# Loads around the attentions' ends moved from SyncE's to ScalarE's DMA queue, output weights in one transfer, all engines in a new order

## The chip, the cores and the metric

The kernel runs on one core of a Trainium2 chip. The metric is the device time of one execution in microseconds. The time before is 1257.52 us, the median of 3 runs (1256.28 to 1263.55). The chip's engines have their own instruction queues and run side by side: PE (TensorE, matmuls), DVE (VectorE), ACT (ScalarE), POOL (GpSimd) and SP (SyncE, which here only issues DMAs). Each engine takes its instructions in the order in which they stand.

## The reference

The reference is one block of a speech encoder with two branches, and the gradients of all its inputs. B = 2 batches, T = 4000 tokens, D = 144 channels, bfloat16.

```python
xa = layernorm(x)
q, k, v = split(xa @ w_qkv)
glob = softmax(q @ k.T * D**-0.5) @ v @ w_att_out
u, g = split(gelu(xa @ w_mlp_in))
loc = (u * depthwise5(layernorm(g), dw_csgu)) @ w_mlp_out
m = concat(glob, loc)
out = x + (m + depthwise5(m, dw_merge)) @ w_merge
# and the gradients of x and of the seven weights for a given grad_out
```

The attention is full: 4000 x 4000 scores in each batch, of which the kernel needs the softmax P and, for the gradients, dP and dS.

## The kernel before

**Tiles.** The tokens of a batch are cut into 32 tiles of 125 queries. `phase_att` runs once for each batch. For tile t it makes the scores in four chunks of 1000 keys (PE, L1046 and L1052), their minimum on the way out of PSUM (DVE, L1070), the exponential (ACT, L1078), the same for dP, which leaves PSUM with a cast on ACT (L1091) and a multiplication on DVE (L1093), or by DVE alone (L1088). P and dS are transposed by DMAs that SP issues: one of P for a whole tile (L1082, called P_tr below) and two halves of dS (L1265). Products with them follow on PE: Y (L1102, from the transposed P), Z (L1140, from the transposed dS) and X (L1185, from both untransposed; DVE adds its results up at L1191). Behind each tile ACT stores a row block of Y and of Z in DRAM (L1117 to `Yn_d`, L1145 to `Zn_d`). The local branch's forward and backward work goes in pieces between the tiles and stores `ug_d` (L633).

**The ends of the attentions.** After the last tile of a batch, class `Merge` does what needs all tokens. `open_early` loads the incoming gradient with its neighbours (`go_h2`) and the stored rows `Yg0` (attention branch) and `Yg1` (local branch); `late_y` loads the last 8 rows of `Yg0` and, in batch 0, starts batch 1's input x; `rem_rows` fills two small stacks `Yr0` and `Yr1`; `open_late` loads `Zn`; `late_w` loads the fused output weights `VU` (two tiles) and `VUs` (two tiles stored once, loaded four times each at shifted positions, over memsets). Matmuls follow:

- `Hps0`, `Hps1` (L1467): the gradient of the merge taps, 384 matmuls; they use the PSUM of the score chunks, and so wait for the last chunks to be read.
- `pz` (L1567): 64 matmuls on `Zn`.
- `po` (L1589, L1591): the output, from `VU`, `VUs` and transposes of Y (SP: L1527, L1535, L1544).
- `dx_a`, `dx_b` (L1604 on ACT, L1618 to L1622): the gradient of x.

In batch 0 the next batch's layernorm, projections and first tiles run into this. I call it the **middle end** (about 535 to 670 us). In batch 1 class `Final` makes the weight gradients at the same time: the **final end** (1125 us to the end).

**Order.** Tables of numbers, one for each engine (`ORDER`, L744 on), set the order of instruction groups; `plan` chains the groups of an engine in that order. SP and ACT each have a DMA queue. All their DMAs share eight semaphores in turn, by the place in the program (named DMAHW0 to DMAHW7 in the rows below): a DMA is issued only when the one eight places earlier that has its semaphore has landed, whichever queue issued that. An engine that waits so holds all that stands behind it.

Of the kernel before, what the change touches and what calls it, by code (L numbers as in the profile page):

```python
# [15 lines left out]
D = 144  # L16
DR = 16
# [94 lines left out]
def end_weights(k, W, pool):  # L112
    eng = k.nc.sync
    W.Wqkv = load_k_(k, pool, k.w_qkv, 0, 3 * D, "Wqkv_e", eng)
    W.Wo = load_k_(k, pool, k.w_att_out, 0, D, "Wo_e", eng)
    W.Wm = [load_k_(k, pool, k.w_merge, h * D, D, "Wm_e%d" % h, eng) for h in range(2)]
    W.Wl = load_k_(k, pool, k.w_mlp_out, 0, D, "Wl_e", eng)
    W.Wvo = unspill(k, pool, W.Wvo_d, "Wvo_e", eng)


def end_taps(k, W, pool):
    eng = k.nc.sync
# [4 lines left out]
class Head:  # L127
# [12 lines left out]
    def wt(self, q, shape):  # L140
        return self.areas[q].tile(shape, BF)
# [153 lines left out]
    def vu(self, h):  # L295
# [4 lines left out]
        if h == 0:  # L300
            W.VU, W.VUs = [], []
# [3 lines left out]
        v = wt(3, [128, 5, D])  # L305
# [6 lines left out]
        W.VU.append(spill(k, v, "VU_d%d" % h))  # L312
        sr = wt(3, [128, 2, 80])
        for ch in range(2):
            for kk in range(5):
                nc.gpsimd.tensor_scalar(sr[:, ch, kk * DR:(kk + 1) * DR], WT[h][:, ch, 128:D], W.cols[:, 2 * h + ch, kk:kk + 1], 1.0, op0=ALU.mult, op1=ALU.mult)
        vs = wt(1, [80, D])
        pt = self.ps([128, D], F32)
        for ch in range(2):
            nc.tensor.matmul(pt[0:80, :], sr[:, ch, :], self.Wm[h][:, ch, :], start=(ch == 0), stop=(ch == 1))  # L320
        nc.scalar.copy(vs, pt[0:80, :])
        W.VUs.append(spill(k, vs, "VUs_d%d" % h))
# [421 lines left out]
for _s in """  # L744
PE 10 1 1 1 1 1 1 1 1 1 1 1 1 1 1 1 1 1 1 1 1 1 1 1 1 1 1 1 1 1 1 1 1 1 1 1 1 1 1 1 1 1 1 1 1 1 1 1 1 1 1 1 1 1 1 1 1 1 1 1 1 1 1 1 1 1 1 1 1 1 1 1 1
# [1337 lines left out]
```

## Time and profile before

| what | before |
|---|---|
| median of 3 runs | 1257.52 us |
| profiled execution | 1252.05 us |
| its span | 1250.3 us |
| PE busy | 1175.9 us (94%) |
| DVE busy | 1042.8 us (83%) |
| ACT busy | 719.9 us (58%) |
| POOL busy | 439.4 us (35%) |
| granted TensorE clock, mean | 0.981 |
| SP's queue, share of 16 DMA engines | 90.9% |
| ACT's queue, share of 16 DMA engines | 2.9% |

The profiled execution's own time is 1.75 us more than its span, and 5.47 us less than the median of the runs. Busy time says little of a single stage: the views used below cut the span into stretches, and name for each wait who waited, for whom and how long. DMA issues have a duration of their own on the queue that issues them (SPq, ACTq), which is not the duration of the transfer.

### The profile page before, as it was taken

How to read it: one execution, taken by the hardware profiler on the slowest of the kernel's cores; microseconds unless marked ns; L12 is line 12 of the kernel's file. 1: busy time of each engine (PE TensorE's matmuls, PEld its weight loads, DVE VectorE, ACT ScalarE, POOL GpSimd, SP SyncE). 2: the span in 40 equal slices, each digit the busy share in tenths (PEclk: the TensorE clock that was granted, in tenths of full speed). 3: DMA queues.
4: the chain of work that ended last, by engine and by line, in shares of the span. 5: the costliest groups of instructions: out<-in, count | busy, mean ns of one | idle time of the engine just before them, and what ended most of it. 6: DMA issues, size and time to landing. Idle time of an engine off the chain costs nothing. (4 is left out here: it accounts for less than half of the span.)

```text
span 1250.3 us, 37996 instructions
## 1 busy us (share of the span) xinstructions
PE 1175.9 (94%) x15384; PEld 923.3 (74%) x15384; DVE 1042.8 (83%) x2846; ACT 719.9 (58%) x1281; POOL 439.4 (35%) x913
## 2 busy tenths in 40 slices
PE   9899999999999999978598999999999999998988
PEld 7566777777777777778576777777777777776877
DVE  7688989898989898856567999989998989896565
ACT  4765666656666665525546666665656556564451
POOL 7543434333443343304124344343433333342100
PEclk9899999999999999989799999999999999999989
DMA  6888899999999999998879999999899999999892
GB/s 133 160 150 148 155 166 162 164 160 164 162 162 162 160 164 164 180 203 161 165 122 164 159 173 156 179 161 164 151 170 156 162 153 162 166 160 182 182 174 75
DMA packets 720027, 200.64 MB, mean 160 GB/s; under 512 B 708365, under 2 KB 716042, under 8 KB 719845
## 3 DMA queue, kind: packets, MB, share of 16 engines
q1 hardware_dynamic: 694326, 190.84, 90.9%
q10 hardware_dynamic: 25348, 7.13, 2.9%
q8 instruction: 120, 1.97, 0.7%
q14 instruction: 57, 0.46, 0.1%
q0 software_dynamic: 176, 0.25, 0.1%
HBM read 22.52 MB, written 16.53 MB: 31 GB/s over the span
## 5 line engine op out<-in xcount | busy, mean ns | idle before, releaser
L1078 ACT ACTIVATE Pb<-Pb,nm 125x1000 bf16<-125x1000 bf16 x256 | 275.2, 1125 | 116.7 <-DVE nm L1072 111.6
L1070 DVE TENSOR_SCALAR_CACHE_REDUCE Pb<-ps 125x1000 bf16<-125x1000 f32 x256 | 306.1, 1196 | 42.5 <-PE ps L1052 40.0
L1185 PE MATMUL X<-SX 125*128 125x144 bf16 x2048 | 292.5, 227 | 0.9 <-ACT l_sq L551 0.7
L1185 PE MATMUL X<-SX,Pb 125*128 125x144 bf16 x2048 | 290.9, 226 | 0.8 <-POOL SX L1131 0.6
L1091 ACT CAST SX<-ps 125x1000 bf16<-125x1000 f32 x189 | 188.1, 995 | 161.7 <-PE ps L1052 158.1
L1046 PE MATMUL ps<-xaT_m,qt 128*128 128x500 bf16 x1024 | 261.1, 375 | 7.7 <-DVE Pb L1070 4.3
L1191 DVE TENSOR_TENSOR acc<-X,acc 125x432 f32<-125x432 f32 x372 | 201.1, 550 | 22.2 <-PE X L1185 21.0
L1185 PEld LDWEIGHTS <-SX 125*128 125x128 bf16 x2048 | 197.6, 98 | 28.2 <-issue 28.2
L1185 PEld LDWEIGHTS <-Pb 125*128 125x128 bf16 x2048 | 200.5, 98 | 2.0 <-issue 1.4
L1140 PE MATMUL yz<-xa_aug,SX 125*128 125x144 bf16 x2048 | 151.0, 228 | 8.2 <-DMA SX<-SX 7.1
L1102 PE MATMUL yz<-xa_aug,SX 125*128 125x145 bf16 x2048 | 144.7, 228 | 10.1 <-DMA SX<-Pb 10.1
L1046 PEld LDWEIGHTS <-qt 128*128 128x128 bf16 x1024 | 91.8, 98 | 71.4 <-issue 8.9
L1102 PEld LDWEIGHTS <-SX 125*128 125x128 bf16 x2048 | 133.4, 98 | 12.7 <-DMA SX<-Pb 11.5
L1140 PEld LDWEIGHTS <-SX 125*128 125x128 bf16 x2048 | 133.2, 98 | 12.7 <-DMA SX<-SX 9.7
L1093 DVE TENSOR_TENSOR SX<-SX,Pb 125x1024 bf16<-125x1024 bf16 x189 | 133.6, 710 | 10.2 <-ACT SX L1091 6.5
L1052 PEld LDWEIGHTS <-qt 16*128 16x128 bf16 x1024 | 26.4, 91 | 110.3 <-issue 110.3
L1052 PE MATMUL ps<-XR,qt 16*128 16x500 bf16 x1024 | 102.9, 380 | 0.0
L1088 DVE TENSOR_TENSOR SX<-ps,Pb 125x1000 bf16<-125x1000 f32 x67 | 79.9, 1193 | 1.2 <-PE ps L1052 1.0
L553 POOL TENSOR_SCALAR l_a<-l_sq 125x576 bf16<-125x576 bf16 x32 | 21.8, 681 | 143.7 <-ACT l_sq L551 143.4
L1129 POOL TENSOR_SCALAR g<-qz,rl 125x144 f32<-125x144 bf16 x62 | 24.9, 401 | 103.2 <-DVE rl L1109 93.7
L1467 PE MATMUL Hps<-Yg,go_h 125*128 125x144 bf16 x640 | 52.7, 232 | 8.6 <-DMA Yg<-Yn_d 8.6
L658 POOL TENSOR_SCALAR l_w<-gdr,nc,c 125x144 f32<-125x144 bf16 x64 | 32.6, 514 | 75.9 <-DVE nc L654 56.5
(593 smaller groups left out, 2041.0 us busy)
## 6 DMA issues: line engine op xcount, KB each, us to landing
go_h<-in_grad_out_dram SPq DMA_DIRECT2D x4, 567.0 KB
go_d<-in_grad_out_dram SPq DMA_DIRECT2D x8, 281.2 KB
Yn_d<-yn ACTq DMA_DIRECT2D x64, 35.2 KB
Zn_d<-qz ACTq DMA_DIRECT2D x64, 35.2 KB
ug_d<-ugr ACTq DMA_DIRECT2D x32, 70.3 KB
out_dram<-Pb SPq DMA_DIRECT2D x16, 140.6 KB
SX<-in_x_dram SPq DMA_DIRECT2D x16, 140.6 KB
out_dram<-SX SPq DMA_DIRECT2D x16, 140.6 KB
```

The lines of the kernel that those rows point to most:

```text
L1046: mm = nc.tensor.matmul(pp[r // 2][:, r % 2, 0:CH], QT[i][:, 3 * h, :], xaTm[:, c * CH:(c + 1) * CH], start=True, stop=False)
L1052: nc.tensor.matmul(pp[r // 2][:, r % 2, 0:CH], QT[i][rs, 1 + h, :], xr, start=False, stop=True)
L1070: nc.vector.tensor_scalar(pv(Pbuf, i % NPB, c2), src, -1.0, 3.0e38, op0=ALU.mult, op1=ALU.min, accum_out=NM[i][:, c2:c2 + 1])
L1078: nc.scalar.activation(v, v, ACT.Exp, bias=NM[i][:, 4:5], scale=-1.0)
L1088: nc.vector.tensor_tensor(pv(Sbuf, i % NDB, c2), src, pv(Pbuf, i % NPB, c2), op=ALU.mult)
L1091: nc.scalar.copy(pv(Sbuf, i % NDB, c2), src)
L1093: nc.vector.tensor_tensor(sc, sc, pchunk(i % NPB, c2), op=ALU.mult)
L1102: nc.tensor.matmul(Y, PT[0:PB, j, :], xaa[:, j, 0:D + 1], start=(j == 0), stop=(j == NB - 1))
L1140: nc.tensor.matmul(Z, ST[0:PB, j, :], xaa[:, j, 0:D], start=(j == 0), stop=(j == NB - 1))
L1185: nc.tensor.matmul(X[:, jj, :], l, r, start=(n_ == 0), stop=(n_ == len(ops) - 1))
L1191: nc.vector.tensor_tensor(av, X[0:PB, 0:nj, :], av, op=ALU.add)
L1467: nc.tensor.matmul(H[a // 6][0:rows, a // 3 % 2, (a % 3) * D:(a % 3 + 1) * D], lhs, self.src[h][:, j, :], start=(j == 0 and a % 3 == 0), s ...
```

## The change

Six places take ScalarE's queue where they took SyncE's: the weights for the final products (`end_weights`, `end_taps`), the loads of `open_early`, `late_y` (with batch 1's x) and `open_late`, and batch 1's gradient. The DMA transposes, the four small copies of `rem_rows`, output stores and copies between DRAM buffers stay on SyncE. The output weights become one tile and one transfer: the kernel's head now computes the shifted copies of `VUs` with four matmul pairs of 128 rows out of a zeroed tile, puts them behind `VU` in one tile for each half and stores that; at each end one load of 128 x 2592 elements (648 KB) takes the place of two loads of 180 KB, eight of 23 KB and two memsets. The order tables of all engines are new.

```diff
 def end_weights(k, W, pool):
-    eng = k.nc.sync
+    eng = k.nc.scalar
 ...
 def end_taps(k, W, pool):
-    eng = k.nc.sync
+    eng = k.nc.scalar
 ...
-        v = wt(3, [128, 5, D])
+            W.VA = k.tc.dram_tile([128, 2, 9, D], BF, name="VA_d")
+            self.va, self.sr = wt(3, [128, 9, D]), wt(3, [128, 2, 232])
+            nc.gpsimd.memset(self.sr, 0.0)
+        v, sr = self.va, self.sr
 ...
-        vs = wt(1, [80, D])
-        pt = self.ps([128, D], F32)
-        for ch in range(2):
-            nc.tensor.matmul(pt[0:80, :], sr[:, ch, :], self.Wm[h][:, ch, :], start=(ch == 0), stop=(ch == 1))
-        nc.scalar.copy(vs, pt[0:80, :])
-        W.VUs.append(spill(k, vs, "VUs_d%d" % h))
+        for q in range(2):
+            pt = self.ps([128, 2 * D], F32)
+            for r in range(2):
+                o = 48 - DR * (2 * q + r)
+                for ch in range(2):
+                    nc.tensor.matmul(pt[:, r * D:(r + 1) * D], sr[:, ch, o:o + 128], self.Wm[h][:, ch, :], start=(ch == 0), stop=(ch == 1))
+            nc.scalar.copy(vf[:, (5 + 2 * q) * D:(7 + 2 * q) * D], pt[:])
+        nc.sync.dma_start(W.VA[:, h], v)
 ...
 # one line of the order tables, before and after (all tables are new)
-Pool 425 -262 23 254 -250 -2 -8 -43 52 -50 298 -297 299 2 -303 40 248 -245 30 -32 68 -4 -56 -44 40 -42 85 -41 9 -2 4 237 -238 -2 245 -151 4 -18 20 1
+Activation 148 1 -4 -1 2 5 -1 -3 81 1 2 1 13 -11 7 -5 14 1 -14 129 -128 1 13 23 10 4 -9 1 80 -78 82 -5 2 -49 46 -36 -5 40 -39 8 37 -7 -36 18 5 19 -15
 ...
     def open_early(self):
 ...
-        eng = nc.sync
+        eng = nc.scalar
 ...
     def late_y(self):
 ...
-        eng = k.nc.sync
+        eng = k.nc.scalar
 ...
     def late_w(self):
-        for h in range(2):
-            self.k.nc.sync.dma_start(self.VU[h], self.W.VU[h][:])
-            self.k.nc.gpsimd.memset(self.VUs[h], 0.0)
-            for r in range(4):
-                self.k.nc.sync.dma_start(self.VUs[h][DR * r:DR * r + 80, r, :], self.W.VUs[h][:])
+        self.k.nc.scalar.dma_start(self.VA, self.W.VA[:])
 ...
-            load_tok(k, self.Zn, 16 * g, S.Zn_d, 16 * g, 16 * g + 16, nc.sync)
+            load_tok(k, self.Zn, 16 * g, S.Zn_d, 16 * g, 16 * g + 16, nc.scalar)
 ...
-    pre_load_go(k, 1, S1, [nc.sync])
+    pre_load_go(k, 1, S1, [nc.scalar])
```

In the rows below, lines of code stand two higher in the changed kernel (L1084 is L1082 before) up to about L1450, and three lower behind it. SP's queue has 605 rows before and 512 after, ACT's 1297 and 1358.

SP around the last transposition of P in the middle end (the row at L1082, or L1084 after), before:

```order
L1265 DMA_TRANSPOSE SX_102<-SX_102 128x16x128 [waits DMAHW5_49,DVE_49,Activation_49]
L51 DMA go_h2_10322<-in_grad_out_dram 112x2592 [waits DMAHW7_49,Pool_49]
L1154 DMA_TRANSPOSE zt_10364<-qz_103 128x2x128 [waits DMAHW0_49]
L42 DMA Yg0_10312<-Yn_d0_79 112x16x144 [waits DMAHW1_49]
L51 DMA go_h2_10322<-in_grad_out_dram 12x2592 [waits DMAHW2_49]
L51 DMA go_h2_10322<-in_grad_out_dram 12x2592 [waits DMAHW4_49]
L1082 DMA_TRANSPOSE SX_102<-Pb_101 128x32x128 [waits DMAHW5_49,PE_49,Activation_49]
L51 DMA go_h2_10322<-in_grad_out_dram 112x2592 [waits DMAHW6_49]
L42 DMA Pb_101<-in_x_dram 112x1152 [waits DMAHW7_49]
```

And after:

```order
L1156 DMA_TRANSPOSE zt_10376<-qz_103 128x2x128 [waits DMAHW7_49,DVE_49]
L1267 DMA_TRANSPOSE SX_102<-SX_102 128x16x128 [waits DMAHW0_49,DVE_49,Activation_49]
L1084 DMA_TRANSPOSE SX_102<-Pb_101 128x32x128 [waits DMAHW1_49,DMAHW6_49,PE_49,Activation_49]
L1578 DMA SX_102<-in_x_dram 125x576 [waits DMAHW5_49,PE_49,Pool_49]
L396 DMA go_d1_85<-in_grad_out_dram 1000x1x144 [waits DMAHW6_49]
L1267 DMA_TRANSPOSE SX_102<-SX_102 128x16x128 [waits DMAHW7_49,DVE_49,PE_49]
L1436 DMA Yr1_10333<-ug_d0_80 124x2x16 [waits DMAHW0_49,Pool_49]
L1436 DMA Yr0_10332<-Yn_d0_79 124x2x16 [waits DMAHW1_49,Pool_49]
```

The four plain loads between a transposition of dS and that of P have left SP.

ACT at the same place. The last cast of a dP chunk (`ps_10381` before, `ps_10393` after) releases `Hps1`'s PSUM and the last half of dS. Before:

```order
L1091 CAST SX_102<-ps_10351 125x8x125 [waits DMAHW3_49,PE_49]
L1078 ACTIVATE Pb_101<-Pb_101,nm_10086 125x8x125
L1117 DMA Yn_d0_79<-yn_10266 125x144 [waits DMAHW4_49,Activation_49]
L1145 DMA Zn_d0_78<-qz_103 125x144 [waits DMAHW6_49]
L1091 CAST SX_102<-ps_10381 125x8x125 [waits PE_49]
L1159 COPY zt_10568<-pt_10569 128x256 [waits PE_49]
```

After, the last 12 of the 24 rows behind the cast of the chunk ahead, up to this cast:

```order
L51 DMA go_h2_10334<-in_grad_out_dram 112x2592 [waits DMAHW0_49]
L42 DMA Pb_101<-in_x_dram 112x1152 [waits DMAHW1_49]
L51 DMA go_h2_10334<-in_grad_out_dram 12x2592 [waits DMAHW2_49]
L1119 DMA Yn_d0_79<-yn_10278 125x144 [waits DMAHW3_49,Activation_49]
L42 DMA Yg0_10324<-Yn_d0_79 112x8x144 [waits DMAHW4_49]
L43 DMA Pb_101<-in_x_dram 13x1152 [waits DMAHW5_49]
L43 DMA Yg1_10325<-ug_d0_80 13x16x144 [waits DMAHW6_49]
L1147 DMA Zn_d0_78<-qz_103 125x144 [waits DMAHW4_49]
L42 DMA Pb_101<-in_grad_out_dram 112x1152 [waits DMAHW5_49,PE_49]
L43 DMA Pb_101<-in_grad_out_dram 13x1152 [waits DMAHW6_49]
L43 DMA Pb_101<-in_grad_out_dram 13x1152 [waits DMAHW7_49]
L1093 CAST SX_102<-ps_10393 125x8x125 [waits PE_49]
```

Two stores stood between the last two casts on ACT before; 23 transfers do after, each with its wait for a landing.

ACT behind the last row block of Z in the middle end, after (these loads stood on SP before, among transposes):

```order
L42 DMA Yg0_10324<-Yn_d0_79 112x8x144 [waits DMAHW5_49,DMAHW1_49]
L43 DMA Yg0_10324<-Yn_d0_79 13x8x144 [waits DMAHW2_49]
L1451 DMA SX_102<-VA_d_986 128x2592 [waits DMAHW3_49,PE_49]
L1147 DMA Zn_d0_78<-qz_103 125x144 [waits DMAHW4_49,DVE_49]
L42 DMA Pb_101<-Zn_d0_78 112x2304 [waits PE_49]
L43 DMA Pb_101<-Zn_d0_78 13x2304 [waits DMAHW6_49]
L1161 COPY zt_10713<-pt_10714 128x256 [waits PE_49]
```

The last rows of `Yg0`, the output weights and the first half of `Zn` now stand around the store of Z's last row block (L1147), in one run of transfers.

More of the change, by code (lines that the diff above doesn't have):

```diff
@@ L300, in vu @@
         if h == 0:
-            W.VU, W.VUs = [], []
             W.sWm_d = [spill(k, sWm[q], "sWm_d%d" % q) for q in range(2)]
@@ L311, in vu @@
             nc.scalar.copy(vf[:, q * 360:(q + 1) * 360], pt[:])
-        W.VU.append(spill(k, v, "VU_d%d" % h))
-        sr = wt(3, [128, 2, 80])
         for ch in range(2):
             for kk in range(5):
-                nc.gpsimd.tensor_scalar(sr[:, ch, kk * DR:(kk + 1) * DR], WT[h][:, ch, 128:D], W.cols[:, 2 * h + ch, kk:kk + 1], 1.0, op0=ALU.mult, op1=ALU.mult)
-        vs = wt(1, [80, D])
-        pt = self.ps([128, D], F32)
-        for ch in range(2):
-            nc.tensor.matmul(pt[0:80, :], sr[:, ch, :], self.Wm[h][:, ch, :], start=(ch == 0), stop=(ch == 1))
-        nc.scalar.copy(vs, pt[0:80, :])
-        W.VUs.append(spill(k, vs, "VUs_d%d" % h))
+                nc.gpsimd.tensor_scalar(sr[:, ch, 48 + kk * DR:48 + (kk + 1) * DR], WT[h][:, ch, 128:D], W.cols[:, 2 * h + ch, kk:kk + 1], 1.0, op0=ALU.mult, op1=ALU.mult)
+        for q in range(2):
[6 more added lines that the diff above has]
+        nc.sync.dma_start(W.VA[:, h], v)
     def conv(self):
@@ L1443, in late_y @@
         o = 16384 + 1024
-        self.VU = [k.SX[:, o + 5 * D * h:o + 5 * D * (h + 1)].rearrange("p (a b) -> p a b", b=D) for h in range(2)]
-        o += 10 * D
-        self.VUs = [k.SX[:, o + 4 * D * h:o + 4 * D * (h + 1)].rearrange("p (a b) -> p a b", b=D) for h in range(2)]
+        self.VA = k.SX[:, o:o + 18 * D].rearrange("p (h a b) -> p h a b", h=2, b=D)
+        self.VU, self.VUs = [self.VA[:, h, 0:5] for h in range(2)], [self.VA[:, h, 5:9] for h in range(2)]
         self.xo = [k.SX[0:PB, q + GB * D * h:q + GB * D * (h + 1)].rearrange("p (a b) -> p a b", b=D) for q in (4096 + 2016, 20480) for h in range(2)]
     def late_w(self):
-        for h in range(2):
-            self.k.nc.sync.dma_start(self.VU[h], self.W.VU[h][:])
-            self.k.nc.gpsimd.memset(self.VUs[h], 0.0)
-            for r in range(4):
-                self.k.nc.sync.dma_start(self.VUs[h][DR * r:DR * r + 80, r, :], self.W.VUs[h][:])
+        self.k.nc.scalar.dma_start(self.VA, self.W.VA[:])
     def open_h(self):
```

3 lines of the change are left out of this document (1 added, 2 removed), and 272 rows, old and new, of the table ORDER.

## The prediction

> **What bounds the kernel now.** I read the stretches of the span first: the head, batch 0's attention, the middle end, batch 1's attention, the final end.
>
> ```profile
> core 0: us, PE busy (x) PEld busy (x) DVE busy (x) ACT busy (x) POOL busy (x), PEclk, DMA share, GB/s
> 0.00:125.00 125.00, 112.03 (x1185) 82.71 (x1186) 97.95 (x269) 78.71 (x158) 64.74 (x156) 0.97 0.79 148
> 125.00:525.00 400.00, 396.46 (x5339) 304.42 (x5337) 364.26 (x940) 246.75 (x376) 153.27 (x306) 1.00 1.01 162
> 535.00:675.00 140.00, 108.59 (x1408) 95.08 (x1405) 84.89 (x296) 65.34 (x169) 34.43 (x72) 0.91 0.91 166
> 675.00:1125.00 450.00, 442.08 (x5886) 338.19 (x5885) 410.84 (x1041) 277.32 (x421) 171.04 (x339) 1.00 0.97 162
> 1125.00:1250.30 125.30, 106.77 (x1454) 95.41 (x1450) 75.77 (x281) 48.54 (x156) 12.81 (x36) 0.94 0.81 153
> ```
>
> The attentions belong to PE: of 850 us it idles 3.5 + 7.9 = 11.5 us. At the ends it idles 31 and 18.5 us, and the granted clock falls. That is where loads can matter. The waits, longest in total first, with total, times and longest in us, name them:
>
> ```profile
> PE yz L1102 <- DMA SX<-Pb: 10.1, 7, 2.3
> PE pz L1567 <- DMA Pb<-Zn_d: 9.7, 2, 4.9
> PE Hps L1467 <- DMA Yg<-Yn_d: 8.6, 2, 5.1
> ```
>
> PE's timeline places them (start, duration, and in brackets the idle time ahead):
>
> ```profile
> 541.33 1.19 PE L1140 MATMUL yz<-xa_aug,SX 125*128 125x144 bf16 x16 [1.58 <-DMA SX<-SX]
> 548.57 2.32 PE L1467 MATMUL Hps<-Yg,go_h 125*128 125x144 bf16 x18 [3.47 <-DMA Yg<-Yn_d]
> 552.43 3.49 PE L1102 MATMUL yz<-xa_aug,SX 125*128 125x145 bf16 x32 [1.54 <-DMA SX<-Pb]
> 579.37 2.08 PE L1467 MATMUL Hps<-Yg,go_h 125*128 125x144 bf16 x16 [5.09 <-DMA Yg<-Yn_d]
> 606.83 5.66 PE L1567 MATMUL pz<-xa_aug,Pb 125*128 125x144 bf16 x64 [4.89 <-DMA Pb<-Zn_d]
> 619.33 0.38 PE L1591 MATMUL po<-SX 128*125 128x144 bf16 x1 [4.65 <-DMA SX<-Yr]
> 1201.63 2.10 PE L1567 MATMUL pz<-xa_aug,Pb 125*128 125x144 bf16 x16 [4.78 <-DMA Pb<-Zn_d]
> 1205.41 0.38 PE L1591 MATMUL po<-SX 128*125 128x144 bf16 x1 [1.08 <-DMA SX<-Yr]
> ```
>
> Whose fault? SP's issues (start, duration on the queue) answer:
>
> ```profile
> 539.03 0.53 SPq L51 DMA_DIRECT2D go_h<-in_grad_out_dram  x1
> ...
> 543.96 6.10 SPq L1082 DMA_TRANSPOSE SX<-Pb  x1
> ...
> 575.13 1.58 SPq L42 DMA_DIRECT2D Yg<-Yn_d  x1
> ...
> 601.28 0.42 SPq L42 DMA_DIRECT2D Pb<-Zn_d  x1
> ...
> 612.98 1.36 SPq L1535 DMA_TRANSPOSE SX<-Yr  x1
> ...
> 1202.04 0.94 SPq L43 DMA_DIRECT2D Pb<-Zn_d  x1
> ```
>
> SP works almost without a break through both ends, and loads go out late because transposes hold the queue for microseconds. Y's last row block was stored by ACT long before SP came to its load at 575.13, and `Zn` was fetched at 601.28:
>
> ```profile
> 557.40 0.27 ACTq L1117 DMA_DIRECT2D Yn_d<-yn  x1
> 569.83 0.26 ACTq L1145 DMA_DIRECT2D Zn_d<-qz  x1
> ```
>
> **The change, term by term.** All terms are against the profiled execution, 1252.05 us; the median of the runs is 5.5 us above it, and I add that at the end.
>
> *Loads behind the last stores, middle end.* ACT now issues the last rows of `Yg0` six rows behind Y's store (L1117 before) and the first half of `Zn` right behind Z's. Before, 17.7 us passed from the store's issue at 557.40 to the load at 575.13, and 31.5 us from 569.83 to 601.28. Even if Y's and Z's last blocks come 8 us later (next term), the loads leave by about 568 and 580. The gaps of 5.09 and 4.89 us go: **-10.0**. What is late next is the following item on PE, and 4.65 us of that was SP's own lateness with the `Yr` stacks. Between 539 and 613 us SP issues 39 plain loads of these kinds (first row quoted above at 539.03), 24.4 us by my sum of their durations, of which the eight `VUs` loads are gone altogether. With over 20 us less ahead of it the transpose at 612.98 should come before it is needed: **-4.6**.
>
> *The last tile, middle end.* This term goes the other way. P_tr leaves SP right after the exponentials, at about 539.4 in place of 543.96, but between ACT's last two dP casts now stand 23 transfers, each waiting for the one eight places ahead to land; one of them waits for P_tr itself. The transfers there and their sizes:
>
> ```profile
> DMA packets 12911, 5.33 MB, mean 213 GB/s; under 512 B 12284, under 2 KB 12284, under 8 KB 12909
> ...
> go_h<-in_grad_out_dram SPq DMA_DIRECT2D x2, 567.0 KB
> Pb<-in_x_dram SPq DMA_DIRECT2D x3, 252.0 KB
> Yg<-Yn_d SPq DMA_DIRECT2D x1, 504.0 KB
> ```
>
> This is the view of DMAs between 535 and 560 us: 213 GB/s with the queues full. Of the 23, those that must have landed before ACT gets to the cast hold some 2.8 MB; P_tr and one half of dS (128 x 4096 and 128 x 2048 elements of 2 bytes) add 1.6 MB. 4.4 MB at 213 GB/s is 20.5 us from 540: the cast runs near 561, where before it ran at 543.72:
>
> ```profile
> 543.72 1.00 ACT L1091 CAST SX<-ps 125x1000 bf16<-125x1000 f32 x1 [4.36 <-PE ps L1052]
> ```
>
> PE meanwhile waits for `go_h2` and P_tr until some 550.5 (idle 5.4 from 545.1), has 54 `Hps0` matmuls and half of Y, about 6 us at the fallen clock, and then waits for the cast until 562: 5.4 + 5.5 = 10.9 us idle against 1.58 + 3.47 + 1.54 = 6.6 now. **+4.3**. Bounds: -2 if nothing but P_tr is waited for, and if all 23 (4.0 MB with P_tr's and the half's 1.6) have to land, 26 us, +10.
>
> *The final end.* `Zn` and the weights leave from ACT, the last 13 rows of `Zn` only behind some forty of ACT's `dx` operations, and one of these loads waits for an output store of SP's. ACT was through nearly all of these operations by 1194 before, while SP sent the last `Zn` rows at 1202.04:
>
> ```profile
> 1192.75 1.30 ACT L1619 ACTIVATE t<-t,dx_c,rstd_x 125x144 f32<-125x144 f32 x3 [0.51 <-DVE t L1618]
> ```
>
>  Of the 4.78 + 1.08 us of waits I take **-4**. The 648 KB of weights go in one piece, 3 us at 213 GB/s, beside `Hps` matmuls. Against it: nine loads stand ahead of the last exponentials, which ran at 1146.24 before, behind an ACT that had been idle:
>
> ```profile
> 1146.24 3.17 ACT L1078 ACTIVATE Pb<-Pb,nm 125x1000 bf16<-125x1000 bf16 x3 [1.56 <-DVE nm L1072]
> ```
>
> Some 3 MB at 213 GB/s from 1133 on is 14 us, so 1147 at best and 1151 with a share for transposes; `Hps` matmuls fill part: **+3** (0 to 8).
>
> *The clock.* Each long gap is followed by slow matmuls:
>
> ```profile
> 550.00:560.00 10.00, 8.46 (x108) 8.16 (x106) 3.93 (x20) 0.65 (x2) 0.66 (x1) 0.74 1.12 254
> ...
> 600.00:610.00 10.00, 4.67 (x49) 4.29 (x49) 4.82 (x20) 6.30 (x19) 0.14 (x2) 0.66 0.87 153
> 610.00:620.00 10.00, 4.80 (x62) 4.05 (x60) 4.27 (x11) 4.96 (x18) 1.16 (x5) 0.83 0.99 195
> 620.00:630.00 10.00, 9.45 (x111) 8.70 (x110) 5.36 (x13) 4.49 (x12) 0.06 (x1) 0.83 0.77 154
> ...
> 1195.00:1205.00 10.00, 4.55 (x48) 4.04 (x47) 3.25 (x14) 2.13 (x6) 0.00 (x0) 0.76 1.00 156
> 1205.00:1215.00 10.00, 9.27 (x101) 8.48 (x102) 6.99 (x19) 7.68 (x20) 0.00 (x0) 0.72 0.94 160
> ```
>
> Busy time times the missing share of the clock: 1.6 + 0.8 + 1.6 behind the gaps of 4.89 and 4.65, 1.1 + 2.6 in the final end, 7.7 in all. The gaps at the front stay, and with them the 2.2 us at 550 to 560. I take three quarters of 7.7: **-6**. The Trainium skill ("TensorE: Matmul & The Clock Gate", Part 1: The HAM clock gate) says that an idle window of about 3.4 us halves the clock and that about 3.4 us of work restores it; by that rule each gap closed below 3.4 us would give back 1.7 us, an estimate, and the four gaps closed here 6.8. The clock of 0.66 to 0.83 in the rows agrees in kind.
>
> *The head.* Twelve small matmuls and two casts more, beside two stores fewer; its PE idles 13 of 125 us. **+0.5** (0 to 3).
>
> *The steady tiles.* All tables are new. They remove no work, so the gain is at most the 11.5 us of PE's idle time there; nothing excludes a loss. I take a quarter of these 11.5 as a loss: **+3** (-5 to +27, see the rivals).
>
> Sum: -10.0 - 4.6 + 4.3 - 4 + 3 - 6 + 0.5 + 3 = -13.8; 1252.05 - 13.8 = 1238, and 1243.5 as a median.
>
> **Rivals.** *The transfer engines are the bound, and the loads land when they did.* The share is 1.12 in the row of 550 to 560, and ACT's transfers wait for SP's by the shared semaphores. Against it: at 600 to 610, where PE waited for `Zn`, the share was 0.87, so there was room. Then the waits of 5.09, 4.89, 4.78 and 1.08 stay with their cold clock; 4.6 and about 2 us of clock are gained, and 4.3 + 3 + 0.5 + 3 lost: 1256, as a median 1262, no change. The Trainium skill has this rule in "DMA: Bandwidth & Descriptors", Issuing engines are not separate DMA queues: DMAs of all queues run on the same 16 engines, and a second issuing queue saves only issue time, usually small beside the transfer. In this trace the issue time isn't small, as the 6.10 us of the transposition of P at 543.96 show; by the page alone I would forecast no change.
>
> *The new order costs the attentions (slower).* Its place is the chain exponential, P_tr, Y, on which PE already waits in the steady tiles. The price of one such wait is 10.1 / 7 = 1.4 us by the first of the waits. If every third of 58 steady tiles has one more, that is 27 us: 1265, as a median 1271, slower by over 1%. It decides from one tile in three on; below, the gain at the ends stands. For it: the order of all engines is drawn anew, and ACT, on which the exponential runs, now can stand for a landing. Against it: PE idles under 1.4% in the attentions now, and nearly all moved loads stand at the ends.
>
> *The casts between ACT's transfers come even later*, with all 23 landed first: +6 on my sum, 1249. This is in the range.
>
> **How the numbers follow.** The forecast has 0.58, the transfer bound 0.22, the slower order 0.20. The forecast's own range is 1230 to 1254: all gaps and the clock gained and the tiles unhurt below, the casts at +10 and half the gains above. A measurement of this kernel can tell about 1%, 12.6 us, from no change: faster means below 1244.9. Two thirds of the forecast's chance lie there (0.38), with 0.02 of the second case; the slower order gives 0.18 and stray cases 0.01; the rest, 0.41, is within 1%. The range of 8 in 10 reaches from 1228 over the transfer bound to 1273.
>
> **What would show each step.** Right: no wait over 2 us of `Hps` for the last `Yg0` rows nor of `pz` for `Zn`; a granted clock above 0.9 from 600 to 630 and from 1200 to 1215; SP with idle stretches after 560; P_tr's issue about 1 us behind the exponentials. The cost: the last dP cast 15 to 20 us behind the one ahead of it, and PE waiting there for ACT. Wrong: `pz` or `po` still waiting for `Zn` or the one weights transfer, most of all in the final end; ACT standing for landings during the attention; or PE idle over 20 us from 125 to 525 and 675 to 1125 together.

## The result, and the profile after

The changed kernel takes 1267.17 us (median of 20 runs), the kernel before 1256.97 us (20 runs): ratio 1.0075, interval 1.0056 to 1.0094, so 0.75% slower. The forecast was 1243.5. The profiled execution after takes 1266.95 us, which is 14.9 more than the 1252.05 of the one before.

The stretches after, in the view by windows (columns as before; the last stretch is 14.8 us longer because the span is):

```profile
0.00:125.00 125.00, 115.45 (x1168) 83.79 (x1169) 98.14 (x265) 80.37 (x161) 65.86 (x157) 0.95 0.80 147
125.00:525.00 400.00, 392.11 (x5270) 300.57 (x5268) 359.99 (x933) 243.01 (x369) 149.06 (x297) 1.00 0.97 159
535.00:675.00 140.00, 109.66 (x1422) 96.35 (x1423) 85.55 (x297) 61.73 (x162) 31.94 (x67) 0.89 0.93 164
675.00:1125.00 450.00, 438.67 (x5782) 334.14 (x5781) 405.69 (x1029) 277.19 (x423) 169.04 (x338) 1.00 0.97 162
1125.00:1265.10 140.10, 118.78 (x1649) 104.76 (x1645) 85.81 (x310) 54.16 (x166) 16.35 (x43) 0.94 0.85 151
```

In the two attentions PE idles 7.9 + 11.3 = 19.2 us, where it idled 11.5 before. The list of waits of PE after has new heads:

```profile
PE Hps L1464 <- DMA go_h<-in_grad_out_dram: 11.2, 1, 11.2
PE ps L1048 <- DVE SX L1090: 9.4, 3, 8.3
PE ps L1048 <- DVE Pb L1072: 6.9, 17, 1.2
PE ps L1048 <- ACT SX L1093: 5.2, 6, 2.6
PE Hps L1464 <- ACT SX L1093: 5.0, 1, 5.0
```

And PE's timeline after places them (columns as before):

```profile
567.37 5.81 PE L1464 MATMUL Hps<-Yg,go_h 125*128 125x144 bf16 x54 [11.18 <-DMA go_h<-in_grad_out_dram]
579.16 0.64 PE L1464 MATMUL Hps<-Yg,go_h 125*128 125x144 bf16 x4 [4.97 <-ACT SX L1093]
...
613.30 0.71 PE L457 MATMUL pt<-ident,xa_aug 125*128 125x125 bf16 x5 [2.32 <-DVE xa_aug L450]
618.85 1.00 PE L457 MATMUL pt<-ident,xa_aug 125*128 125x125 bf16 x8 [3.77 <-DVE acc L1193]
...
1154.88 0.58 PE L1048 MATMUL ps<-xaT_m,qt 128*128 128x500 bf16 x2 [2.58 <-ACT SX L1093]
1170.58 0.99 PE L1048 MATMUL ps<-xaT_m,qt 128*128 128x500 bf16 x2 [8.33 <-DVE SX L1090]
```

All that the change was credited with came true as a wait: `Hps` no longer waits for the last `Yg0` rows, `pz` not for `Zn`, `po` not for the `Yr` stacks. But the middle end's long gaps are 11.18 + 4.97 + 2.32 + 3.77 = 22.2 us now, and were 6.6 + 5.09 + 4.89 + 4.65 = 21.2: the waits stand ahead of `Hps` in place of behind it. In the final end the gaps moved into the last tile's scores.

The timelines of ACT and SP, put together in order of time, show what the front of the middle end waits for:

```profile
547.50 0.98 ACT L1093 CAST SX<-ps 125x1000 bf16<-125x1000 f32 x1
...
547.63 7.75 SPq L1084 DMA_TRANSPOSE SX<-Pb  x1
...
551.73 1.37 ACTq L43 DMA_DIRECT2D Yg<-ug_d  x1
561.74 0.81 ACTq L42 DMA_DIRECT2D Pb<-in_x_dram  x2
562.59 0.40 ACTq L51 DMA_DIRECT2D go_h<-in_grad_out_dram  x1
...
578.12 0.99 ACT L1093 CAST SX<-ps 125x1000 bf16<-125x1000 f32 x1 [29.64 <-DMA Zn_d<-qz]
```

P_tr leaves SP at 547.63. By its listed waits ACT's load of x has to wait for the transfer eight places ahead of it, which is this transposition, and it leaves at 561.74, 14.1 us behind. A load of `go_h` that the first `Hps` matmul needs (the last 12 of 124 rows of one half) stands behind it and leaves at 562.59; the matmul starts 4.8 us behind that. So the transfers on ACT's queue are not free of SP's: each has one of eight completion counters, and the counters are shared by both queues. The last cast comes 30.6 us behind the one ahead of it.

To compare kernels I cut each trace where the score matmuls of a tile end (tiles counted over both batches, 64 in all). us in each stretch, worked out from the traces:

| stretch | before | after | after, second trace |
|---|---|---|---|
| tile 4 to 28 (batch 0, steady) | 379.2 | 387.0 | 388.5 |
| 28 to 32 | 69.2 | 71.5 | 72.8 |
| 32 to 36 (middle end) | 158.4 | 156.0 | 154.2 |
| 36 to 60 (batch 1, steady) | 381.0 | 383.3 | 384.5 |
| 60 to 64 (last tiles) | 69.4 | 80.2 | 85.2 |
| 64 to the last matmul (final end) | 92.1 | 86.3 | 86.2 |

The steady tiles lose 7.8 + 2.3 us. The other four rows gain 2.4 + 5.8 and lose 2.3 + 10.8: 4.9 us lost, where the forecast's terms for the ends and the clock were 17.3 gained.

### The profile page after: what moved, and what is told of

The parts are those of the page before. It is cut to its first block, busy times and chain, and to the rows that moved or that the text cites. A ratio compares the mean times of both kernels' runs of the same rounds, so it can differ in the third digit from the quotient of the medians.

```text
span 1265.1 us, 38001 instructions
## 1 busy us (share of the span) xinstructions
PE 1184.0 (94%) x15396; PEld 926.8 (73%) x15396; DVE 1041.8 (82%) x2846; ACT 720.5 (57%) x1283; POOL 437.6 (35%) x910
## 4 chain that ended last, share of the span: by engine, by line
PE 58%; DVE 16%; DMA 12%; ACT 5%; issue 3%; POOL 2%; ACTq 2%; SPq 1%; DVEq 0%; POOLq 0%
PE X L1187 14%; PE ps L1048 12%; PE yz L1104 7%; PE yz L1142 6%; DVE Pb L1072 5%; PE ps L1054 5%; DMA SX<-Pb 3%; DMA SX<-SX 3%; PE po L1586 2%; DVE acc L1193 2%; ACT Pb L1080 2%; PE Hps L1464 1%; PE warm L154 1%; DMA out_dram<-Pb 1%; DVE SX L1095 1%
## 5 line engine op out<-in xcount | busy, mean ns | idle before, releaser
L1048 PE MATMUL ps<-xaT_m,qt 128*128 128x500 bf16 x1024 | 264.8, 377 | 23.0 <-DVE SX L1090 9.4
L1048 PEld LDWEIGHTS <-qt 128*128 128x128 bf16 x1024 | 92.4, 98 | 87.4 <-issue 28.9
L1095 DVE TENSOR_TENSOR SX<-SX,Pb 125x1024 bf16<-125x1024 bf16 x189 | 132.6, 705 | 11.8 <-ACT SX L1093 11.6
L1054 PEld LDWEIGHTS <-qt 16*128 16x128 bf16 x1024 | 26.5, 91 | 111.7 <-issue 111.7
L1464 PE MATMUL Hps<-Yg,go_h 125*128 125x144 bf16 x640 | 55.5, 239 | 16.1 <-DMA go_h<-in_grad_out_dram 11.2
L1131 POOL TENSOR_SCALAR g<-qz,rl 125x144 f32<-125x144 bf16 x62 | 25.4, 409 | 104.6 <-DVE rl L1111 98.1
L1464 PEld LDWEIGHTS <-go_h 125*128 125x128 bf16 x640 | 47.2, 105 | 16.6 <-DMA go_h<-in_grad_out_dram 11.3
```

The costliest lines, as they stand in the source:

```text
L1048: mm = nc.tensor.matmul(pp[r // 2][:, r % 2, 0:CH], QT[i][:, 3 * h, :], xaTm[:, c * CH:(c + 1) * CH], start=True, stop=False)
L1054: nc.tensor.matmul(pp[r // 2][:, r % 2, 0:CH], QT[i][rs, 1 + h, :], xr, start=False, stop=True)
L1095: nc.vector.tensor_tensor(sc, sc, pchunk(i % NPB, c2), op=ALU.mult)
L1464: nc.tensor.matmul(H[a // 6][0:rows, a // 3 % 2, (a % 3) * D:(a % 3 + 1) * D], lhs, self.src[h][:, j, :], start=(j == 0 and a % 3 == 0), s ...
```

## Experiments

Three theories stood first: ACT stands for landings with work of the last tiles behind it (1); loads on ACT's queue slow SP's transposes (2); the new order of the steady tiles is the loss (3). In the expectations "ratio" is the time against the kernel before.

### The order by itself, and the queue by itself

**The changed order with the loads on SP:**

```diff
 def end_weights(k, W, pool):
-    eng = k.nc.scalar
+    eng = k.nc.sync
 ...
-        self.k.nc.scalar.dma_start(self.VA, self.W.VA[:])
+        self.k.nc.sync.dma_start(self.VA, self.W.VA[:])
 ...
+# the moved loads stand in SP's table where they stand in the program
```

> The changed kernel, its order of all engines and its one transfer of output weights kept, with all plain loads back on SP's queue, each put into SP's row where it stands in the changed program. Theory 1 (ACT's standing is the loss): ACT's last cast and last exponentials come on time, SP is as full as before, so the late loads return; the time is 5 to 10 us under the changed kernel, ratio 0.997 to 1.003 against before. Theory 3 (the order is the loss): the steady tiles stay 8 us slower (S of tile 4 to S of tile 28 in 387 us instead of 379) and the time stays at 1.005 or above. Theory 2: P_tr in the middle end lands within 9 us of its issue, as before, where the changed kernel took 14.

1266.73 us, ratio 1.0075 (1.005 to 1.0099): as slow as the whole change. ACT no longer stands for these loads, and the last tiles are as short as before (60 to 64: 67.4), but `Hps` waits for the loads at both ends, in PE's list of waits:

```profile
PE Hps L1468 <- DMA go_h<-in_grad_out_dram: 14.4, 1, 14.4
PE Hps L1468 <- DMA xaT_m<-in_w_merge_dram: 13.7, 1, 13.7
```

The final end is 98.1 us long in place of 86.3. What the queue gains there, it loses in the last tiles.

**The queue with the order of before** (`VU` and `VUs` kept as they were):

```diff
 def end_weights(k, W, pool):
-    eng = k.nc.sync
+    eng = k.nc.scalar
 ...
+# before's tables; each of 71 loads in ACT's table where ACT stood at its issue time
```

> The kernel before, its order of all engines and its output weights in ten loads kept, with the 71 plain loads of open_early, late_y, open_late, end_weights, end_taps and batch 1's gradient issued by ACT's queue, each put into ACT's row at the place at which SP issued it in the trace of before. Theory 1: those loads that stand ahead of ACT's casts and exponentials make ACT wait, those behind the last stores come sooner; the waits of 5.09 and 4.89 us for Yg0 and Zn shrink, the last casts come late: between -8 and +6 us against before. Theory 3 (the new order is the loss): without it the queue alone gives what was forecast at the ends, 10 to 15 us faster than before, ratio 0.988 to 0.992. Theory 2: slower than before by 3 to 8 us, since P_tr shares the transfer engines with a second queue.

1267.52 us, ratio 1.0076 (1.0051 to 1.0101). The steady tiles are as before (380.8 and 379.6); the loss is in the ends, 169.6 us from tile 32 to 36 and 100.1 behind tile 64. So the moved loads alone, at places on ACT that differ from the change's, cost as much as the whole change.

### What stands behind the loads on ACT

**The changed kernel, the last dP cast of the middle end ahead of the 23 transfers:**

```diff
+# ACT's table: the cast at L1093 of the middle end's last dP chunk
+_put('Activation', [3151], 3120)
```

> The changed kernel with one row moved: in the middle end ACT's last cast of a dP chunk (L1093, ps_10393) stands ahead of the 23 transfers, right behind the cast before it. Theory 1 (ACT stands in its queue for landings, and what stands behind it is late): the 29.6 us between the two casts fall below 3 us, PE's wait of 4.97 us for the cast goes, the second half of dS leaves SP some 20 us earlier, and the time falls by 5 to 9 us against the changed kernel, to a ratio near 1.002 against before. Theory 2 (the transfers on ACT's queue slow the transposes, whatever ACT does meanwhile): the wait of Hps for go_h2 of 11.18 us and P_tr's 14 us from issue to landing stay, and the time falls by less than 3 us. Theory 3 (the loss is the new order of the steady tiles): nothing at the end matters, ratio 1.0075 as the changed kernel.

1269.81 us, ratio 1.0103 (1.0078 to 1.0127). PE's wait for the cast is gone, and nothing came of it:

```profile
PE Hps L1471 <- DMA go_h<-in_grad_out_dram: 11.9, 1, 11.9
...
PE pt L457 <- DVE acc L1200: 5.2, 1, 5.2
PE Hps L1471 <- POOL go_r L1427: 4.5, 1, 4.5
```

POOL's copy `go_r` needs all of `go_h` and takes the cast's place as a wait. But the moved cast stands for PE's scores itself and runs at 554.13, 7.0 us behind the one ahead of it where less than 3 was expected, and the loads behind it leave 7 us later than in the changed kernel (the first at 554.14, there 547.15). So the run trades one stand of ACT for another: it shows that the loads of `go_h` are late with the cast gone as a wait, not how late they are without either stand.

**The changed kernel, `yn`, exponentials and casts of the last tile ahead of the nine loads of the final end:**

```diff
+_put('Activation', [6303, 6341, 6342, 6340, 6345, 6343, 6353], 6331)
```

> The changed kernel with seven rows of ACT moved: in the final end the last exponentials (L1080), the row block of Y ahead of them (L1118) and the last two casts (L1093) stand ahead of nine loads instead of behind them. Theory 1: ACT's wait of 13.07 us ahead of that row block goes, the last score chunk ends near 1160 instead of 1173.8, PE's wait of 8.33 us there shrinks below 2; the loads leave later, so Hps waits for them 3 to 5 us; the time falls by 3 to 8 us against the changed kernel. Theory 2: P_tr and the dS transposes beside the loads stay slow, and what is gained ahead of the score chunk is lost again at Hps: within 2 us of the changed kernel. Theory 3: no change.

1275.35 us, ratio 1.0148 (1.0116 to 1.0181), the slowest of all. The last scores end at 1157.7 in place of 1173.8, and then `Hps` waits for the loads:

```profile
PE Hps L1471 <- DMA xaT_m<-in_w_merge_dram: 19.8, 1, 19.8
```

**The changed kernel, the cast first and three `go_h` loads ahead of batch 1's x loads:**

```diff
+_put('Activation', [3151], 3120)
+_put('Activation', [3119, 3125, 3126], 3195)
```

> The changed kernel with the middle end's last dP cast ahead of ACT's transfers (as in the run with the cast first) and with the three loads of output gradients that Hps waited for ahead of batch 1's x loads on ACT. If the wait of 11.18 us comes from place in ACT's queue, behind loads that stand for P_tr by the shared semaphores: that wait falls to 0 to 3 us, the middle end becomes 8 to 10 us shorter, ratio about 1.000. If it comes from the transfer engines being full (loads land no sooner from any place): the wait stays above 8 us or goes to other loads of the same stretch, and the ratio stays 1.006 to 1.010.

1267.95 us, ratio 1.0089 (1.0057 to 1.012). The wait for `go_h` stays at 9.6 us; 8.2 us of another came up behind it:

```profile
PE Hps L1472 <- DMA go_h<-in_grad_out_dram: 9.6, 1, 9.6
PE X L1195 <- DVE SX L1133: 8.2, 1, 8.2
```

ACT's timeline shows why this run doesn't decide between the place in the queue and the transfers themselves:

```profile
554.48 0.99 ACT L1101 CAST SX<-ps 125x1000 bf16<-125x1000 f32 x1 [6.19 <-PE ps L1062]
...
560.52 1.23 ACTq L51 DMA_DIRECT2D go_h<-in_grad_out_dram  x3
```

As in the run with the cast first, the cast stands 6.2 us for PE and holds every load behind it. The three `go_h` loads leave at 560.52, directly behind the loads ahead of them, and so only 2.1 us earlier than the first of them did in the changed kernel (562.59). PE's wait ends at 565.92, 5.4 us behind that issue (4.8 in the changed kernel). So in these two kernels the wait follows the time at which the load leaves, and the expected 0 to 3 us for an early place was not put to the test.

The other theory of that expectation, full transfer engines, stays open too. They are busy nearly all the time around there, but at 190 to 211 GB/s, where the kernel before moved 254 GB/s from 550 to 560. The windows of the changed kernel (the last two columns are the DMA share and GB/s, the one ahead the granted clock):

```profile
550.00:560.00 10.00, 5.70 (x76) 4.47 (x73) 4.93 (x10) 0.00 (x0) 0.34 (x1) 0.92 1.28 190
560.00:570.00 10.00, 2.63 (x23) 2.63 (x24) 0.31 (x1) 0.00 (x0) 0.00 (x0) 0.50 0.93 211
570.00:580.00 10.00, 5.03 (x58) 4.90 (x57) 4.78 (x22) 0.99 (x1) 1.35 (x3) 0.84 1.14 197
...
600.00:610.00 10.00, 10.00 (x164) 10.00 (x162) 5.72 (x35) 8.39 (x30) 4.03 (x8) 1.00 0.68 146
610.00:620.00 10.00, 3.91 (x41) 3.11 (x39) 8.30 (x37) 6.41 (x19) 2.94 (x8) 0.65 0.87 162
...
1165.00:1175.00 10.00, 3.74 (x19) 1.76 (x19) 3.29 (x6) 6.52 (x8) 2.96 (x8) 0.55 1.14 167
...
1205.00:1215.00 10.00, 9.11 (x141) 8.36 (x139) 7.80 (x45) 8.62 (x39) 0.11 (x1) 1.00 0.94 256
```

**The changed kernel with long rows.** The loads that fill `Yg0`'s first 24 rows and `Yg1` read the output gradient, in long runs:

```diff
-            load_tok(k, self.src[0], 16 * g, self.tok(0), 16 * g, 16 + 8 * g, eng)
-            load_tok(k, self.src[1], 16 * g, self.tok(1), 16 * g, 16 * g + 16, eng)
+            row = tok_view(k.go, b)
+            load_tok(k, self.src[0], 16 * g, row, 16 * g, 16 + 8 * g, eng)
+            load_tok(k, self.src[1], 16 * g, row, 16 * g, 16 * g + 16, eng)
```

> The changed kernel, with its order, queues and bytes, but the eight transfers at each end that fill Yg0's first 24 rows and Yg1 read rows of the output gradient, which lie in DRAM in runs of 4608 or 6912 bytes, in place of rows of Yn_d and ug_d, which lie in runs of 288 bytes (so the products made of Y and U are not the reference's). If these many short packets on ACT's queue are what slows SP's transposes and so makes ACT stand at both ends: the last two dS transposes of the final end take 8 us on SP's queue in place of 13.4, P_tr's in the middle end 6 in place of 7.8, ACT's stands of 29.6 and 13.1 us become 20 and 5, the kernel 8 to 14 us shorter, ratio 0.997 to 1.002. If the volume alone or the place in the queue counts: the stands stay above 25 and 11 us, ratio 1.005 to 1.009.

1272.35 us, ratio 1.0123 (1.0096 to 1.0149), above both expected ranges. Of ACT's two stands one is 4.6 us shorter than in the first trace of the changed kernel (29.6), the other 10.0 longer (13.1), in ACT's list of waits:

```profile
ACT SX L1093 <- DMA Yg<-in_grad_out_dram: 25.0, 1, 25.0
ACT yn L1118 <- DMA Yg<-in_grad_out_dram: 23.1, 1, 23.1
```

SP's transposes are no faster: P_tr of the middle end holds the queue 10.4 us (7.8 in the changed kernel, 6 expected), the last two of dS in the final end 23.0 (13.4, 8 expected). The many packets of 288 bytes are not what makes these late.

**The changed kernel once more**, for a second trace:

> The changed kernel once more, for a second trace of it: steady stretch 386 to 388 if that loss is the order's; the last two dS transposes of the final end between 11 and 25 us on SP's queue, and the stretch from tile 60 to the last matmul between 164 and 176, if what stands there differs from execution to execution.

1274.12 us (two runs), ratio 1.0129 (1.0086 to 1.0173). The run with long rows, 1.0123, was compared with the same executions of the kernel before and is level with it. The steady stretch is 388.5 us, so that loss is stable. What is not stable is the last tile. SP's own waits between 1140 and 1180 us, in the first trace and in the second:

```profile
SPq L1267 <- DMA SX<-SX: 5.5, 1, 5.5
```

```profile
SPq L1267 <- DMA SX<-SX: 18.5, 1, 18.5
```

The transposition of dS's second half waits on SP for a landing which, by its name, is that of the first half's, and beside ACT's loads this takes 13 us more in one execution than in the other. ACT stood 13.1 us there in the first trace, and 20.3 in the second.

### The credited loads alone

**The kernel before, with the last two pairs of `Yg0` loads and the four `Zn` loads sent from ACT behind the last stores:**

```diff
-            load_tok(k, self.src[0], 16 * g, self.tok(0), 16 * g, 16 + 8 * g, eng)
+            load_tok(k, self.src[0], 16 * g, self.tok(0), 16 * g, 16 + 8 * g, (nc.sync, nc.scalar)[g])
 ...
-        load_tok(k, self.src[0], 24, self.tok(0), 24, 32, eng)
+        load_tok(k, self.src[0], 24, self.tok(0), 24, 32, k.nc.scalar)
 ...
-            load_tok(k, self.Zn, 16 * g, S.Zn_d, 16 * g, 16 * g + 16, nc.sync)
+            load_tok(k, self.Zn, 16 * g, S.Zn_d, 16 * g, 16 * g + 16, nc.scalar)
 ...
+# these loads leave SP's table and stand behind the last stores of Y and of Z in ACT's
```

> The kernel before with one part of the change alone: at both ends the last two pairs of loads of Y's rows go out from ACT right behind Y's last store, and the four Zn loads from ACT behind Z's last store; SP keeps everything else, in its old order. If the terms of the prediction for these loads are right (gaps of 5.09, 4.89 and 4.78 us and the cold clock behind them): 8 to 18 us faster than the kernel before, ratio 0.986 to 0.994. If the transfer engines are the bound, or the next item on PE (the Yr stacks, P_tr) is late by as much: ratio 0.997 to 1.003. If loads on a second queue slow what SP still issues: above 1.003.

1257.30 us, ratio 1.0012 (0.9987 to 1.0037): no gain. The gaps of 5.09 and 4.89 us are gone, and PE's timeline has these in their place:

```profile
590.55 0.47 PE L455 MATMUL pt<-ident,xa_aug 125*128 125x125 bf16 x3 [3.73 <-ACT t L1624]
593.77 0.70 PE L455 MATMUL pt<-ident,xa_aug 125*128 125x125 bf16 x5 [2.74 <-DVE xa_aug L448]
600.24 1.00 PE L455 MATMUL pt<-ident,xa_aug 125*128 125x125 bf16 x8 [3.26 <-DVE acc L1196]
...
618.49 0.38 PE L1596 MATMUL po<-SX 128*125 128x144 bf16 x1 [4.91 <-DMA SX<-Yr]
```

The transposes of batch 1's tokens, which PE has to do before `pz`, need DVE and ACT, and these are not ready earlier: `pz` starts at 605.69, where it started at 606.83. `Zn` was late beside something else that was as late.

### The order of the steady tiles

**The changed kernel with before's order in tiles 4 to 28 and 38 to 58** (all five engines; loads and ends stay the change's). Here and below the edit is in the tables alone, so no diff is shown.

> The changed kernel, but tiles 4 to 28 of batch 0 and 38 to 58 of the 64 score tiles counted over both batches have the order of before on all five engines; ends and loads stay the change's. Theory 3 (the new order of the steady tiles is the loss): from the end of tile 4 to that of tile 28, 387.0 us in the changed kernel falls back to 379 to 381, and in batch 1 another 1 to 2 go; the kernel takes 1257 to 1259, ratio about 1.000 to the kernel before. Theory 1 and 2 (ACT's standing at the ends, slowed transposes): the stretch may stay at 385 or above, or what is gained there is lost at the ends; ratio 1.006 to 1.008.

1268.6 us, ratio 1.0076 (1.0047 to 1.0104). The stretch fell back to 379.8 us as theory 3 had it, but the whole did not: tiles 36 to 60 took 386.3, and tiles 60 to 64 took 86.0. In the first there is one long stand of ACT in tile 45, which the timeline shows with SP's transposition of P ahead of it:

```profile
827.74 7.05 SPq L948 DMA_TRANSPOSE SX<-Pb  x1
...
838.42 0.26 ACTq L1011 DMA_DIRECT2D Zn_d<-qz  x1
838.72 1.26 ACT L620 COPY gT<-pt 128x625 bf16<-128x625 bf16 x2 [5.63 <-DVE SX L954]
```

A store of Z stood ahead of the copy until 838.42, and PE idled 3 us behind it. The 86.0 is the unsteady last tile again. So I took the two windows and the queue apart.

**The same, with tiles 4 to 28 alone:**

> The changed kernel with the order of before in tiles 4 to 28 of batch 0 alone; batch 1, where the run with both windows had one stall of a store on ACT, keeps the changed order. Theory: the new order of the steady tiles costs 7 to 8 us in batch 0 and little in batch 1, and the ends trade even. Then: that stretch 379 to 381, batch 1's tiles 36 to 60 between 382 and 385 as in the changed kernel, ratio 1.000 to 1.003. Rival: whatever is gained there is taken back by the ends, whose loads stand on ACT; then ratio 1.005 to 1.008.

1261.11 us, ratio 1.0034 (1.0009 to 1.006): 4.1 thousandths, some 5 us, less than the changed kernel. The stretch is 378.2; 9 us are gained in it, and 4 go again in tiles 36 to 60 (387.3, where the same order took 383.3 in the changed kernel): a store stands as in the run ahead, and here the trace names what it stood for, the landing of P's transposition:

```profile
832.66 1.26 ACT L620 COPY gT<-pt 128x625 bf16<-128x625 bf16 x2 [3.55 <-DMA SX<-Pb]
```

**Both windows, and the loads on SP:**

> The changed kernel with both suspects taken out: the plain loads back on SP (as in the run with the order alone) and the tiles 4 to 28 and 38 to 58 in the order of before. If the steady order and the loads on ACT's queue are the loss, each by itself: steady stretch 379 to 381, final end as in the run with the order alone (165.5 from tile 60 to the last matmul), ratio 1.000 to 1.003. If what is gained in the steady tiles is lost again behind them, as in the run with the steady order: ratio 1.005 to 1.009.

1257.27 us, ratio 1.0000 (0.9978 to 1.0021): the loss is gone. Against the run with the order alone, 1.0075, only the two windows differ. Against the run with both windows and the loads on ACT, 1.0076, only the queue differs. So with the old steady order the loads on ACT cost 0.76% by themselves. The one transfer of the output weights and the new order of the ends are still in this version, and cost nothing that shows in sum.

**The kernel before with the new order in tiles 6 to 27 of batch 0, and nothing else:**

> The kernel before with one part of the change alone: the five engines' new order in tiles 6 to 27 of batch 0 (21 of the 24 tiles of the stretch); everything else, queues and weights too, as before. If the new order of the steady tiles costs by itself: 6 to 7 us more from tile 4 to 28 (385 to 386), ratio 1.004 to 1.007. If it costs only together with loads on ACT: 379 to 381, ratio 0.998 to 1.002.

1263.39 us, ratio 1.0056 (1.0036 to 1.0076): one part of the change, without a load moved, costs 7 us. The stretch from tile 4 to 28 in the kernel before, the changed kernel, the changed kernel with the window put back, and this one (first column: from and to; then length, PE busy):

```profile
95.30:474.50 379.20, 373.31 (x4950) 286.59 (x4950) 344.34 (x878) 237.02 (x362) 144.83 (x291) 1.00 0.99 161
```

```profile
95.80:482.80 387.00, 375.65 (x4954) 287.31 (x4950) 345.12 (x879) 237.49 (x362) 146.69 (x291) 1.00 0.95 158
```

```profile
93.50:471.70 378.20, 373.44 (x4950) 286.52 (x4950) 344.89 (x879) 237.06 (x362) 146.49 (x292) 1.00 0.97 160
```

```profile
96.00:482.40 386.40, 375.14 (x4950) 287.32 (x4950) 344.27 (x878) 237.72 (x362) 145.34 (x291) 1.00 0.97 158
```

The same matmuls, at the same clock, with 5.4 us more idle time of PE (11.3 in place of 5.9) and 1.8 us more of busy time. The idle time is in 26 pieces, none above 2 us. Of the waits with a name, PE's list for that stretch gives DVE's most: before, and in this run:

```profile
PE ps L1046 <- DVE Pb L1070: 1.8, 7, 0.6
```

```profile
PE ps L910 <- DVE Pb L934: 3.8, 9, 1.2
PE ps L910 <- DMA qt<-qz: 2.0, 1, 2.0
```

The next tile's scores wait longer for DVE to read the scores ahead of them out of PSUM, but this is 2.0 of the 5.4 us; the rest is spread over several waits. Which engine's table does it was not taken apart. Nor was the one transfer of the output weights tried by itself. No version of these beats the kernel before.

## Why the prediction was wrong

The sign was wrong: 14 us faster was forecast, 10 us slower was measured. The time is inside the range, 1228 to 1273, by its upper part, which was drawn for the rivals. The rival of the slower order came near it in number (1271) by another mechanism, which is luck. Between the two profiled executions the change cost 14.9 us, so the miss against the sum of -13.8 is 28.7 us. By the table of stretches some 22 of it lie in the terms for the ends and the clock (17.3 gained in the forecast, 4.9 lost) and some 7 in the steady tiles (3 lost in the forecast, 10.1 measured). Point by point:

- *Loads behind the last stores, -10.0, and SP's lateness, -4.6.* Each of the waits went away, and PE's time didn't. The failed step is "What is late next is the following item on PE, and 4.65 us of that was SP's own lateness": I asked only which load was late next. The runs showed DVE's and ACT's work for batch 1's tokens right behind (3.73, 2.74 and 3.26 us in the run with the credited loads alone), so those loads were worth nothing, 1.0012. The wait for the `Yr` stacks stayed in that run (4.91), so the -4.6 was not tried by itself. A wait removed is worth the distance to the next one, and the next one must be sought on every engine.
- *The last tile, middle end, +4.3.* The mechanism was right, the term mis-sized. The cast came 30.6 us behind the one ahead where 15 to 20 were forecast, and PE's idle time there is 11.18 + 4.97 = 16.2 us against 10.9 forecast: +9.6 against 6.6 before, just inside the upper bound. The rate was near the 213 GB/s that I took: between P_tr's issue and the cast the engines moved 6.07 MB at 199 GB/s. The volume was too small: I counted 4.4 MB as needed, and 5.6 MB (26 us) as the most. And a rate is not the whole of it, since each transfer stands for another's landing; P_tr took 14.1 us to let the next load go. The two runs with the cast first put another stand in the place of this one, so what the middle end would take without it is not shown.
- *The final end, -4 and +3.* Both mechanisms were there. The stretch behind tile 64 is 5.8 us shorter; the second term was far too small. The exponentials stood 13.1 us behind the nine loads (20.3 in the second trace), and tiles 60 to 64 grew by 10.8 us (15.8).
- *The clock, -6.* The clock rose where gaps had been, from 0.66 to 1.00 in the row of 600 to 610 and from 0.72 to 1.00 in that of 1205 to 1215, and fell where they went: 0.50, 0.65 and 0.55 in the rows of 560, 610 and 1165 us above.
- *The head, +0.5.* As forecast in the first trace; other executions lie 4 us apart there, so nothing rests on it.
- *The steady tiles, +3.* +10.1 was measured (7.8 + 2.3), in the part that I called unhurt but for a guess. It was shown from both sides: put back, the old order gains 9 us in batch 0's stretch; the new one, added to the kernel before, costs 7. The rival of the slower order had the right place in the program and the wrong mechanism: not one more P_tr wait in every third tile, but many waits of under 2 us, those of the score matmuls for DVE first among them.

Taken together, the steady order and the queue make a table of four kernels, all with the new order at the ends (ratio to the kernel before, with its interval):

| steady tiles | loads on SP | loads on ACT |
|---|---|---|
| order of before | 1.0000 (0.9978 to 1.0021) | 1.0076 (1.0047 to 1.0104) |
| new order | 1.0075 (1.005 to 1.0099) | 1.0075 (1.0056 to 1.0094) |

Each of the two parts costs the whole 0.75% when it comes alone, and both together cost no more than one. So the loss can't be divided between them: taking out either by itself does not get the time back, as the run with both windows and the run with the order alone show, and taking out both does. The queue with the order of before throughout, 1.0076, says the same of the loads. The run with batch 0's window alone, 1.0034 (1.0009 to 1.006), lies between; its interval overlaps that of the run with both windows.

Why they don't add up is open. The stretches say where the queue's cost falls: with the old steady order, the version with the loads on ACT takes 7.2 us more than that with the loads on SP in tiles 36 to 60 (386.3 against 379.1), 19.5 more in the last tiles (86.0 against 66.5), and gains 14.4 back in the final end (88.0 against 102.4). With the new order the trade is even: 12.8 lost in the last tiles, 11.8 gained behind them. These are single executions, and some 4 us between two of them mean little: the kernel before with nothing but the order of tiles 6 to 27 changed has a final end of 96.4 us, where the kernel before has 92.1.

The rival that the transfer engines bound the ends is not shown, only in agreement with the time of two kernels: in the new order the loads take as long on SP as on ACT. The rule quoted from the Trainium skill ("DMA: Bandwidth & Descriptors", Issuing engines are not separate DMA queues) agrees with that. In the old steady order the queue is not indifferent, 1.0000 against 1.0076, and there the trace shows ACT standing 5.63 us in tile 45, behind a store, and 20.5 us in the last tiles, for the landing of a load. The 6 us of issue time that made me doubt the rule were real, but they were hidden behind other late work.

What stays open besides: which engine's table makes the steady order slower, and whether `go_h` would come in time from a place on ACT with no stand ahead of it.

## What to carry to other kernels

Before a wait is credited, list what else on the waiting engine is not ready at that time, on all engines, and credit the distance to the latest of them. Loads that go to the queue of a computing engine take place in that engine's order: every cast, exponential and store behind them waits for the landings that the loads wait for, and through shared completion counters these can be the other queue's transposes. And when a change redraws the order of tiles that it doesn't touch, run that part by itself first: here it cost 0.56% without a load moved. When two parts are under suspicion, run all four combinations: here either part alone accounts for the whole loss.

## What the runs showed of the hardware

- How long a transposition by DMA takes to land beside loads of another queue differs much from one execution of the same program to the next: SP waited 5.5 us for the first half of dS in one trace of the changed kernel, 18.5 in another.
- Loading with rows of 4608 bytes and more in place of 288 made the transposes beside them no faster (10.4 us against 7.8 and 7.4 in two executions for P_tr on SP's queue, 23.0 against 13.4 and 26.5 for the last two of dS), and ACT stood 25.0 and 23.1 us, against 29.6 and 13.1 in one execution, 28.9 and 20.3 in the other.
- At the front of the middle end PE waited 11.2 us for `go_h` from ACT's queue, 14.4 from SP's, and 9.6 with three of its loads put ahead behind a cast that stood 6.2 us for PE. In the first and the last of these PE started 4.8 and 5.4 us behind the issue of the load that it needed, so the time went into the standing ahead of the issue.
